# Window attention and two feed-forward layers: the second layer's first product by one level of Strassen's algorithm

## The chip, the core and the metric

The kernel runs on one core of a Trainium2 chip. Its engines have instruction streams of their own and meet at semaphores: TensorE (PE, with its weight loads as PEld) multiplies matrices into PSUM, VectorE (DVE) and ScalarE (ACT) work element by element, GpSimd (POOL) makes constants at the start, and SyncE (SP) issues every DMA transfer. The metric is the device time in microseconds, the median of several runs.

## What is computed

```
q, k, v: (4, 8, 576, 64)     windowed attention, window 64
x = attention output as (2304, 512)
x = relu(x @ w_in1)^2 @ w_out1       w_in1 (512, 2048), w_out1 (2048, 512)
y = elu(x @ w_in2) @ w_out2          w_in2 (512, 2048), w_out2 (2048, 512)
```

q, k and v are 32-bit floats, the four weights 64-bit floats. The output is (2304, 512) in 32-bit floats.

## The kernel before

**Numbers.** Each operand of a large product is split into a high and a low half (`split`, lines 110 to 113: ScalarE writes the high half, VectorE subtracts it for the low one), and each product is three matmuls: high by high, high by low, low by high (`mm3`, lines 289 to 294). Weights come as pairs of 32-bit words. `w_load` (129 to 133) fetches 512 KB for one 128-wide slice, `w_split` (135 to 159) makes a float of it with one ScalarE and four VectorE instructions of 512 columns and splits it. The raw words and the split weight take turns in one buffer, so a load waits for the last matmul that used that buffer.

**Tiles and loops.** The tokens go in five blocks of 512, 256, 512, 512 and 512, numbered 0 to 4. d_ff is cut into 16 slices j. `m_h` (296 to 325) multiplies a block by one slice of w_in into one of two PSUM banks (`ph`), applies the activation (relu squared in layer one; in layer two min on VectorE, exp on ScalarE, max on VectorE) and splits the result into `gs`. `m_out` (327 to 358) adds the slice's part of the second product to four PSUM accumulators (o0 to o3), two slices behind `m_h` (LA = 2). Layer one writes its output to DRAM (`x2d`, through `ev` tiles), layer two reads it back (`x_load`, `x_split`). In layer two the accumulators hold 128 tokens by 512 outputs each, so that block 1, which comes last there (ORDER2), uses two of them.

**Attention** of block t + 1 is done during block t of layer one, a head pair at a time: `u_S` (208 to 245) makes scores, masks, exp and scaling, `u_V` (247 to 269) transposes, multiplies by v and splits into `xs`. The loop spreads it: scores at every third slice, v two slices later. Its loads are issued one head pair ahead.

**Weights by due time.** All weights of layer one are decoded during attention and block 0, those of layer two during block 4 and the first block of layer two; `due` (393 to 397) says how many by when, and `load_w` issues the loads two per slice:

```
    def due(i):

        if i < NJ:
            return min(2 * (LA + 2) + 2 * i, 2 * NJ)
        return 2 * NJ + max(0, (20 * (i - LAST)) // 16)
```

**Order.** The code gives instructions in program order; a scheduler with a timeline of its own then sets the order on each engine, subject to the buffers of each tag (pb 4, pt and ev together 3, y 3, gs 3).

## Time and profile before

| | us |
|---|---|
| median of 3 runs | 891.06 (888.93 to 892.03) |
| profiled run | 890.37 |
| its span, first to last instruction | 888.6 |
| TensorE busy | 870.0 |
| VectorE busy | 503.6 |
| ScalarE busy | 373.8 |
| mean granted TensorE clock | 0.998 of full |

The profiled run has 1.8 us outside its span. The page gives busy times and cuts the span into 40 slices of 22 us; the views by stretch give the same for any interval, with the clock that TensorE was granted. A matmul's own duration includes the way through the array: matmuls overlap, so their cost in a row is read from the starts of groups in the timeline, not from their mean duration.

### The profile page before, as it was taken

To read this page: it belongs to the slowest core of one execution; us is meant where nothing else is said; L and a number is where in the kernel's file an instruction comes from. 1 tells how busy PE (TensorE), PEld (TensorE's weight loads), DVE (VectorE), ACT (ScalarE), POOL (GpSimd) and SP (SyncE) were. 2 spreads that over 40 slices of the span, in tenths; PEclk is the share of its full clock that TensorE was granted. 3 is DMA by queue.
4 is the path that set the end of the run, shared out by engine and by line. 5 is a ranking of instruction groups with operands and counts; after the bars stand their busy time and mean duration, and the time that the engine had idled before them with its cause. 6 is when DMAs were issued, how large, how long until landed. Compare 5 with 4: busy or idle time off the path is not lost.

```text
span 888.6 us, 12491 instructions
## 1 busy us (share of the span) xinstructions
PE 870.0 (98%) x4752; PEld 732.2 (82%) x4752; DVE 503.6 (57%) x1269; ACT 373.8 (42%) x848; POOL 6.9 (1%) x27
## 2 busy tenths in 40 slices
PE   6799999999999999999999999999999999999998
PEld 5488889998888888888888888888888888888897
DVE  6999994435444344444999994543354334433343
ACT  6777765434334243433566542322232223222232
POOL 3000000000000000000000000000000000000000
PEclk9999999999999999999999999999999999999999
DMA  9991212221112111015666400110001000100000
GB/s 267 379 365 38 76 49 78 70 73 50 50 50 56 65 50 49 25 54 185 197 200 195 142 0 1 48 48 1 0 24 48 1 0 1 48 1 0 33 16 24
DMA packets 43835, 67.91 MB, mean 76 GB/s; under 512 B 21504, under 2 KB 24064, under 8 KB 43776
## 3 DMA queue, kind: packets, MB, share of 16 engines
q1 hardware_dynamic: 43776, 67.12, 23.4%
q8 instruction: 37, 0.61, 0.3%
q14 instruction: 22, 0.18, 0.1%
HBM read 57.67 MB, written 9.44 MB: 76 GB/s over the span
## 4 chain that ended last, share of the span: by engine, by line
PE 96%; DVE 3%; DMA 0%; issue 0%; SPq 0%
PE ph L292 44%; PE o L292 44%; PE pa L218 3%; PE pa L264 2%; PE pa L256 1%; DVE pb L242 1%; PE po L218 1%; DVE pb L226 1%; DVE y L154 0%; DVE y L151 0%; DMA kr<-in_k_dram 0%; DVE w L113 0%; DVE xs L113 0%; DVE y L144 0%; DVE y L147 0%
## 5 line engine op out<-in xcount | busy, mean ns | idle before, releaser
L292 PE MATMUL ph<-xs,w 128*128 128x512 f32 (+1 forms) x1920 | 434.0, 371 | 3.7 <-ACT xs L112 2.1
L292 PEld LDWEIGHTS ph<-xs,w 128*128 128x128 f32 x1920 | 336.8, 189 | 66.3 <-ACT xs L112 2.4
L292 PE MATMUL o<-gs,w 128*128 128x512 f32 (+1 forms) x960 | 215.3, 371 | 0.0
L292 PE MATMUL o<-w,gs 128*128 128x512 f32 x864 | 209.6, 389 | 0.0
L292 PEld LDWEIGHTS o<-gs,w 128*128 128x128 f32 x960 | 166.9, 188 | 29.0
L292 PEld LDWEIGHTS o<-w,gs 128*128 128x128 f32 x864 | 161.1, 188 | 32.7
L113 DVE TENSOR_TENSOR gs<-g,gs 128x512 fp32r<-128x512 f32 (+1 forms) x160 | 101.9, 637 | 73.0 <-ACT gs L112 72.8
L112 ACT ACTIVATE gs<-g 128x512 fp32r<-128x512 f32 (+1 forms) x160 | 93.8, 588 | 85.7 <-DVE g L321 55.7
L320 ACT ACTIVATE g<-g 128x512 f32<-128x512 f32 (+1 forms) x80 | 47.1, 589 | 192.5 <-DVE g L317 192.5
L317 DVE TENSOR_SCALAR g<-ph 128x512 f32<-128x512 f32 (+1 forms) x80 | 51.0, 638 | 100.5 <-PE ph L292 100.3
L311 ACT ACTIVATE g<-ph 128x512 f32<-128x512 f32 (+1 forms) x80 | 44.1, 554 | 96.5 <-PE ph L292 95.8
L315 DVE TENSOR_TENSOR g<-g 128x512 f32<-128x512 f32 (+1 forms) x64 | 39.9, 624 | 69.3 <-ACT g L311 69.2
L321 DVE SCALAR_TENSOR_TENSOR g<-g,ph 128x512 f32<-128x512 f32 (+1 forms) x80 | 50.7, 634 | 46.3 <-ACT g L320 46.3
L231 ACT ACTIVATE pb<-pb,nm 128x128 f32<-128x128 f32 x144 | 55.9, 390 | 23.3 <-DVE nm L226 23.2
L143 ACT ACTIVATE y<-wraw 128x512 f32<-128x512 f32 x64 | 42.6, 672 | 25.8 <-DVE w L113 18.5
L112 ACT ACTIVATE w<-y 128x512 fp32r<-128x512 f32 x64 | 39.9, 628 | 17.4 <-DVE y L154 17.3
L113 DVE TENSOR_TENSOR w<-y,w 128x512 fp32r<-128x512 f32 x64 | 43.8, 686 | 0.2 <-ACT w L112 0.2
L151 DVE SCALAR_TENSOR_TENSOR y<-wraw,y 128x512 uint32<-128x512 uint32 x64 | 43.6, 687 | 0.1
L154 DVE SCALAR_TENSOR_TENSOR y<-wraw,y 128x512 uint32<-128x512 uint32 x64 | 43.4, 686 | 0.1
L113 DVE TENSOR_TENSOR xs<-pa,xs 128x512 fp32r<-128x512 f32 (+1 forms) x20 | 12.7, 636 | 42.9 <-ACT xs L112 42.8
L242 DVE TENSOR_SCALAR pb<-pb,rc 128x128 f32<-128x128 f32 x144 | 31.6, 282 | 0.7
L218 PEld LDWEIGHTS pa<-kr,qd 128*128 128x128 f32 x224 | 28.6, 191 | 1.8
(36 smaller groups left out, 368.8 us busy)
## 6 DMA issues: line engine op xcount, KB each, us to landing
wraw<-in_moe_w_in_dram SPq DMA_DIRECT2D x32, 512.0 KB, 5.0
wraw<-in_moe_w_out_dram SPq DMA_DIRECT2D x32, 512.0 KB, 5.3
vr<-in_v_dram SPq DMA_DIRECT2D x16, 512.0 KB, 4.1
out_dram<-ev SPq DMA_DIRECT2D x18, 256.0 KB, 2.1
qd<-in_q_dram SPq DMA_DIRECT2D x32, 128.0 KB, 3.3
x2d<-ev SPq DMA_DIRECT2D x16, 256.0 KB, 2.5
xr<-x2d SPq DMA_DIRECT2D x8, 512.0 KB, 3.5
kr<-in_k_dram SPq DMA_DIRECT2D x12, 288.0 KB, 3.4
```

Source lines behind the costliest of these rows:

```text
L112: nc.scalar.activation(out=hi, in_=x, func=AF.Copy)
L113: eng.tensor_tensor(out=lo, in0=x, in1=hi.bitcast(F32), op=ALU.subtract)
L143: nc.scalar.activation(out=yf, in_=upper.bitcast(F32), func=AF.Abs)
L151: nc.vector.scalar_tensor_tensor(out=y, in0=upper, scalar=0xC0000000, in1=y, op0=ALU.bitwise_and, op1=ALU.bitwise_or)
L154: nc.vector.scalar_tensor_tensor(out=y, in0=lower, scalar=29, in1=y, op0=ALU.logical_shift_right, op1=ALU.bitwise_or)
L218: nc.tensor.matmul(out=ps[:, i * P:(i + 1) * P], lhsT=qr[:, b0 + i].rearrange("p a x -> p (a x)"), rhs=kr[:, o:o + P], start=True, stop=True,)
L231: nc.scalar.activation(out=pb[:, c], in_=pb[:, c], func=AF.Exp, bias=nm[:, b:b + 1], scale=-1.0, accum_out=sm[:, b:b + 1],)
L292: nc.tensor.matmul(out=ps, lhsT=a[x], rhs=b[y], start=(first and i == 0), stop=(last and i == 2))
L311: nc.scalar.activation(out=g[:, :n], in_=ps[:, :n], func=AF.Relu)
L317: nc.vector.tensor_scalar(out=g[:, :n], in0=ps[:, :n], scalar1=0.0, scalar2=None, op0=ALU.min)
L320: nc.scalar.activation(out=g[:, :n], in_=g[:, :n], func=AF.Exp)
L321: nc.vector.scalar_tensor_tensor(out=g[:, :n], in0=g[:, :n], scalar=-1.0, in1=ps[:, :n], op0=ALU.add, op1=ALU.max)
```

## The change

The first product of layer two is computed with the Winograd form of Strassen's algorithm, one level. The tokens of layer two now go in three stripes s of 768, each of two halves of 384 (HALF). d_model is halved too, and a pair i of slices (2i, 2i + 1) makes the two halves of the third dimension. For each of 3 x 8 pairs, seven products of (256 x 128) by (256 x 384) take the place of eight. A product is two chunks of 128 by three matmuls of 384 columns: 24 x 42 = 1008 matmuls of 384 columns, where there were 768 of 512 and 192 of 256. The second product has as many columns as before, all in matmuls of 512.

- **Weight side.** `w_sums(r)` makes the seven left operands of a pair: it decodes two w_in slices, makes four sums of 256 columns, splits seven operands and writes them to DRAM (`wop`), 1.83 MB a pair. It is called eight times in layer one, every six slices from block 1 on; the raw slices and the operands share two "stage" buffers of 512 KB. `wo_load` brings a pair's operands back for each stripe, in the buffers of the attention's `xs`.
- **Token side.** `x_sums` and `x_op` make the seven right operands of a stripe in the buffers of layer one's w_in; for stripe 0 in block 4, for a later one in the last pair of the stripe before.
- **The pair.** Seven products go through two PSUM banks. ScalarE copies the first and the third result, VectorE adds the others up with u2 and u3, which use the "y" buffers of the decode. Four results (384 tokens by 128) go through the activation. The 36 output matmuls of a pair stand between the products of the next one; six accumulators are used (o0 to o3 and the two attention banks). The outputs of layer one's last two slices stand between the products of pair (0, 0).
- **Buffers.** pb 4 to 3, pt with ev 3 to 2, y 3 to 2. The decode of w_out of layer two is due one slice of weights per j in block 4, and the last ones in pair (0, 0).

```diff
-ORDER2 = [0, 2, 3, 4, 1]
+HALF = 384
...
-        y = sc.tile([P, KD * P], U32, tag="y", name="y", bufs=3)
+        y = sc.tile([P, KD * P], U32, tag="y", name="y", bufs=2)
...
+    def w_sums(i):
...
+        add, sub = ALU.add, ALU.subtract
+        H = KD * P // 2
+        y0, y1 = w_float(1, 2 * i, 0), w_float(1, 2 * i + 1, 0)
+        a11, a12, a21, a22 = y0[:, :H], y0[:, H:], y1[:, :H], y1[:, H:]
...
+        nc.vector.tensor_tensor(out=s1, in0=a21, in1=a22, op=add)
+        nc.vector.tensor_tensor(out=s2, in0=s1, in1=a11, op=sub)
+        nc.vector.tensor_tensor(out=a21, in0=a11, in1=a21, op=sub)
+        nc.vector.tensor_tensor(out=s4, in0=a12, in1=s2, op=sub)
+        for k, xs_ in enumerate(((a11, s2), (a12, a21), (s1, a22), (s4,))):
+            n = len(xs_)
+            w = wts.tile([P, 2, 2, 2, P], F32R, tag="stage", name="wo", bufs=2)
...
+            nc.sync.dma_start(out=wop[i][k][:, :n], in_=w[:, :n].bitcast(F32))
...
+    def wo_load(s, i):
...
+            w = xp.tile([P, 2, 2, 2, P], F32R, tag=f"xs{k}", name="wo")
+            nc.sync.dma_start(out=w[:, :n].bitcast(F32), in_=wop[i][k][:, :n])
...
-            pb = at.tile([P, 4 * P], F32, tag="pb", name="pb", bufs=4)
+            pb = at.tile([P, 4 * P], F32, tag="pb", name="pb", bufs=3)
...
-            pt = at.tile([P, 512], F32, tag="pt", name="pt", bufs=3)
+            pt = at.tile([P, 512], F32, tag="pt", name="pt", bufs=2)
...
+    def x_op(s, k):
...
+            src = (b11, t2[c], b21, b12, t1[:, c, :], b21, b22)[k]
+            o = wts.tile([P, 2, HALF], F32R, tag=f"w{2 * k + c}0", name="xo")
+            split(o[:, 0, :], o[:, 1, :], src, nc.vector)
...
+                e = at.tile([P, 512], F32, tag="pt", name="ev", bufs=2)
...
+        a = bank()
+        product(a, 0, A11, True, True)
+        m1 = keep("pb", 3)
+        copy(m1, a[:, :HALF], nc.scalar)
+        after(0)
+        b = bank()
+        product(b, 1, S2, True, True)
+        u2 = plus(keep("y", 2, sc), b, m1)
+        after(1)
+        product(a, 2, A12, False, True)
+        c = keep("pb", 3)
+        copy(c, a[:, :HALF], nc.scalar)
+        out[0, 0] = elu(c)
+        after(2)
+        b = bank()
+        product(b, 3, S3, True, True)
+        u3 = plus(keep("y", 2, sc), b, u2)
+        after(3)
+        a = bank()
+        product(a, 4, S1, True, True)
+        out[1, 1] = elu(plus(keep("pb", 3), a, u3))
+        after(4)
+        product(b, 5, A22, False, True)
+        out[1, 0] = elu(plus(keep("pb", 3), b, u2))
+        after(5)
+        product(a, 6, S4, False, True)
+        out[0, 1] = elu(plus(keep("pb", 3), a, u2))
+        after(6)
...
-    wseq = [(L, j, i) for L in range(2) for j in range(NJ) for i in range(2)]
+    wseq = [(0, j, i) for j in range(NJ) for i in range(2)] + [(1, j, 1) for j in range(NJ)]
...
-        return 2 * NJ + max(0, (20 * (i - LAST)) // 16)
+        return 2 * NJ + max(0, i - LAST)
...
+        if i < len(its) - 2:
+            for f in outs:
+                f()
+        else:
+            left += outs
+        if t == NB - 1:
+            load_w(2 * NJ + j)
+            if j == 0:
+                x_load(0)
+                wo_load(0, 0)
+            elif j == 1:
+                x_sums(0)
+            if j >= 2:
+                x_op(0, (j - 2) // 2) if j % 2 == 0 else None
...
+        r, m = divmod(i - NJ, 6)
+        if r in range(NI):
+            if m == 0:
+                w_load(1, 2 * r, 0)
+            elif m == 2:
+                w_load(1, 2 * r + 1, 0)
+            elif m == 5:
+                w_sums(r)
...
+    for s in range(NS):
+        for i in range(NI):
+            if (s, i) != (NS - 1, NI - 1):
+                wo_load(*divmod(s * NI + i + 1, NI))
+            if s + 1 < NS and i == 3:
+                x_load(s + 1)
+            if s + 1 < NS and i == NI - 1:
+                x_sums(s + 1)
...
+            def after(k, s=s, i=i, fs=left):
+                for f in spread(fs, k):
+                    f()
+                if s == 0 and i == 0:
+                    decode(wd[0] + 1)
+                if s + 1 < NS and i == NI - 1:
+                    x_op(s + 1, k)
...
+            left = pair_out(s, i, pair(s, i, after))
```

Three places show what the scheduler makes of it. In the rows, a name's number tells buffers apart; "x3" stands for three such instructions; what a row waits for is in brackets.

TensorE at the start of layer two, before. ph_4908 is the slice's first product, o0 to o3 the accumulators of the first block, gs_4762 the activation of slice 0:

```order
L292 MATMUL o0_4874<-w_4222,gs_4762 128x512 [waits DVE_49]
L292 MATMUL o2_4876<-w_4222,gs_4762 128x512
L292 MATMUL o1_4875<-w_4222,gs_4762 128x512 [waits DVE_49]
L292 MATMUL o1_4875<-w_4222,gs_4762 128x512 x2
L292 MATMUL ph_4908<-xs_4244,w_4413 128x512 [waits DVE_49]
L292 MATMUL ph_4908<-xs_4244,w_4413 128x512 x2
L292 MATMUL ph_4908<-xs_4388,w_4413 128x512 x3
L292 MATMUL ph_4908<-xs_4532,w_4413 128x512 x3
```

TensorE there after; the last outputs of layer one's slices are past. ph_5221 and ph_5209 are the two banks, and their rows the fifth, sixth and seventh product of pair (0, 0); xo are the token operands, wo the weight operands, gs_5203 the pair's first activation:

```order
L377 MATMUL o0_5291<-w_4573,gs_5203 128x512 [waits DVE_49]
L377 MATMUL o1_5292<-w_4573,gs_5203 128x512
L377 MATMUL o2_5293<-w_4573,gs_5203 128x512
L377 MATMUL ph_5221<-xo_4971,wo_4523 128x384 [waits DMAHW2_49,DVE_49]
L377 MATMUL ph_5221<-xo_4971,wo_4523 128x384 x2
L377 MATMUL ph_5221<-xo_4974,wo_4523 128x384 x3
L377 MATMUL ph_5209<-xo_5062,wo_4523 128x384 [waits DVE_49]
L377 MATMUL ph_5209<-xo_5062,wo_4523 128x384 x2
L377 MATMUL ph_5209<-xo_5066,wo_4523 128x384 x3
L377 MATMUL ph_5221<-xo_5122,wo_4525 128x384 [waits DMAHW3_49,DVE_49]
```

The outputs of the first activation still come first, but no output stands between the products that follow: three come in a row, each behind a wait for VectorE.

VectorE at the start of layer two, before. y is the float of a weight in the making, g the activation:

```order
L151 SCALAR_TENSOR_TENSOR y_5066<-wraw_4637,y_5066 128x512 [waits DVE_49]
L113 TENSOR_TENSOR w_5031<-y_5025,w_5031 128x512 [waits Activation_49]
L317 TENSOR_SCALAR g_4863<-ph_4850 128x512 [waits PE_49]
L144 TENSOR_SCALAR y_5075<-y_5075 128x512 [waits Activation_49]
L113 TENSOR_TENSOR gs_4807<-g_4806,gs_4807 128x512 [waits Activation_49]
L154 SCALAR_TENSOR_TENSOR y_5066<-wraw_4637,y_5066 128x512 [waits DVE_49]
L144 TENSOR_SCALAR y_5116<-y_5116 128x512 [waits Activation_49]
L147 TENSOR_SCALAR y_5075<-y_5075 128x512 [waits DVE_49]
L321 SCALAR_TENSOR_TENSOR g_4863<-g_4863,ph_4850 128x512 [waits Activation_49]
```

VectorE there after. y_5170 is the last w_out slice in the making, y_5186 is u2 and y_5216 is u3:

```order
L163 SCALAR_TENSOR_TENSOR y_5139<-wraw_5137,y_5139 128x512 [waits DVE_49]
L153 TENSOR_SCALAR y_5170<-y_5170 128x512 [waits Activation_49]
L156 TENSOR_SCALAR y_5170<-y_5170 128x512 [waits DVE_49]
L119 TENSOR_TENSOR w_5145<-y_5139,w_5145 128x512 [waits Activation_49]
L160 SCALAR_TENSOR_TENSOR y_5170<-wraw_5148,y_5170 128x512 [waits DMAHW2_49,DVE_49]
L465 TENSOR_TENSOR y_5186<-ph_5179,pb_5165 128x384 [waits DVE_49]
L163 SCALAR_TENSOR_TENSOR y_5170<-wraw_5148,y_5170 128x512 [waits DVE_49]
L119 TENSOR_TENSOR w_5176<-y_5170,w_5176 128x512 [waits Activation_49]
L465 TENSOR_TENSOR y_5216<-ph_5209,y_5186 128x384 [waits DVE_49,PE_49]
```

Before, the activation's steps and those of the decode alternate. After, u2 stands behind three steps of the decode of wraw_5148, u3 behind two more.

TensorE at the end of block 1, before, from just behind the last head pair's products with v. xs_2261 is that pair's result, ph_2338 and ph_2369 the first products of block 2, o0_1636 to o3_1639 the outputs of block 1:

```order
L292 MATMUL ph_2338<-xs_1909,w_395 128x512
L292 MATMUL ph_2338<-xs_2085,w_395 128x512 x3
L292 MATMUL o0_1636<-gs_2290,w_1411 128x256
L292 MATMUL o0_1636<-gs_2290,w_1411 128x256 [waits DVE_49]
L292 MATMUL o0_1636<-gs_2290,w_1411 128x256
L292 MATMUL o1_1637<-gs_2290,w_1411 128x256 x3
L292 MATMUL o2_1638<-gs_2290,w_1411 128x256 x3
L292 MATMUL o3_1639<-gs_2290,w_1411 128x256 x3
L292 MATMUL ph_2369<-xs_1733,w_568 128x512 [waits Activation_49]
L292 MATMUL ph_2369<-xs_1733,w_568 128x512 x2
L292 MATMUL ph_2369<-xs_1909,w_568 128x512 x3
L292 MATMUL ph_2338<-xs_2261,w_395 128x512 [waits Activation_49]
```

TensorE there after. xs_2340 is the last head pair's result, pa the attention's banks, ph_2458 the first product of block 2:

```order
L377 MATMUL o2_1670<-gs_2441,w_1492 128x256
L377 MATMUL o3_1671<-gs_2441,w_1492 128x256 x3
L304 MATMUL pa_2309<-ident_81,pb_2212 128x128 [waits DVE_49] x4
L304 MATMUL pa_2316<-ident_81,pb_2232 128x128 [waits DVE_49]
L312 MATMUL pa_2323<-pt_2314,vr_2022 64x64 [waits DMAHW0_49,Activation_49]
L312 MATMUL pa_2323<-pt_2314,vr_2022 64x64 x7
L304 MATMUL pa_2316<-ident_81,pb_2232 128x128 [waits DVE_49] x3
L312 MATMUL pa_2323<-pt_2321,vr_2022 64x64 [waits Activation_49]
L312 MATMUL pa_2323<-pt_2321,vr_2022 64x64 x7
L266 MATMUL pa_2562<-kr_2200,qd0_84 128x128 [waits DMAHW3_49,DMAHW4_49,DMAHW2_49,PE_49]
L266 MATMUL pa_2562<-kr_2200,qd0_84 128x128 x3
L377 MATMUL ph_2458<-xs_2340,w_427 128x512 [waits Activation_49]
```

Before, twelve matmuls of outputs and ten of products stood between the last head pair's v products and the first use of its result. After, only the next scores (pa_2562) do, and the outputs of block 1 stand ahead of the head pair's transposes.

## Rows read from the trace of the kernel before

**Rows 1.** The page: busy time of the engines, then 40 slices of the span: tenths of VectorE busy, and GB/s moved by DMA.
```profile
PE 870.0 (98%) x4752; PEld 732.2 (82%) x4752; DVE 503.6 (57%) x1269; ACT 373.8 (42%) x848; POOL 6.9 (1%) x27
...
DVE  6999994435444344444999994543354334433343
...
GB/s 267 379 365 38 76 49 78 70 73 50 50 50 56 65 50 49 25 54 185 197 200 195 142 0 1 48 48 1 0 24 48 1 0 1 48 1 0 33 16 24
```

**Rows 2.** Busy time by stretch: from and to, length, busy us (and instructions) of PE, PEld, DVE, ACT and POOL, granted clock of TensorE, share of the DMA engines, GB/s.
```profile
10.00:20.00 10.00, 7.19 (x75) 6.18 (x75) 9.63 (x67) 9.27 (x40) 0.00 (x0) 1.00 1.11 309
...
30.00:40.00 10.00, 8.02 (x82) 5.30 (x78) 10.00 (x27) 5.67 (x11) 0.00 (x0) 1.00 1.04 385
...
50.00:60.00 10.00, 10.00 (x46) 8.29 (x45) 10.00 (x25) 5.98 (x14) 0.00 (x0) 1.00 1.03 414
...
90.00:100.00 10.00, 10.00 (x47) 8.28 (x47) 9.96 (x25) 6.56 (x13) 0.00 (x0) 1.00 0.11 34
...
200.00:300.00 100.00, 100.00 (x602) 83.91 (x601) 42.28 (x151) 39.08 (x112) 0.00 (x0) 1.00 0.18 50
...
430.00:500.00 70.00, 70.00 (x310) 57.99 (x309) 69.54 (x134) 43.04 (x73) 0.00 (x0) 1.00 0.63 198
```

**Rows 3.** Waits of TensorE over the whole span: what waited, for what, us in total, times, longest.
```profile
PE po L218 <- DMA kr<-in_k_dram: 7.2, 3, 5.8
PE ph L292 <- ACT xs L112: 2.1, 2, 1.4
```

**Rows 4.** Timeline of TensorE in layer two, 499 to 510 us: start, length from the first start to the last end, and the group.
```profile
501.40 2.88 PE L292 MATMUL ph<-xs,w 128*128 128x512 f32 x12
504.12 3.56 PE L292 MATMUL o<-w,gs 128*128 128x512 f32 x15
```

**Rows 5.** The same view in layer two's last block, of 256 tokens.
```profile
862.02 1.60 PE L292 MATMUL ph<-xs,w 128*128 128x256 f32 x12
863.45 1.55 PE L292 MATMUL o<-w,gs 128*128 128x512 f32 x6
864.84 1.60 PE L292 MATMUL ph<-xs,w 128*128 128x256 f32 x12
```

**Rows 6.** TensorE's groups by form, both layers: busy us, mean ns of one, idle before.
```profile
L292 PE MATMUL ph<-xs,w 128*128 128x512 f32 x1536 | 380.8, 393 | 3.7 <-ACT xs L112 2.1 <-DVE xs L113 1.1 <-DVE w L113 0.5
L292 PE MATMUL o<-w,gs 128*128 128x512 f32 x864 | 209.6, 389 | 0.0
...
L292 PE MATMUL ph<-xs,w 128*128 128x256 f32 x384 | 53.3, 285 | 0.0
```

**Rows 7.** Groups by form of VectorE, then of ScalarE, same columns.
```profile
L113 DVE TENSOR_TENSOR gs<-g,gs 128x512 fp32r<-128x512 f32 x128 | 88.4, 691 | 58.5 <-ACT gs L112 58.2
...
L144 DVE TENSOR_SCALAR y<-y 128x512 f32<-128x512 f32 x64 | 26.8, 423 | 5.0 <-ACT y L143 4.8
...
L226 DVE CUSTOM_DVE_ANT_0 pb<-pa,mask 128x128 f32<-128x128 f32 x112 | 25.8, 286 | 4.2 <-PE pa L218 4.1
L113 DVE TENSOR_TENSOR gs<-g,gs 128x256 fp32r<-128x256 f32 x32 | 13.6, 425 | 14.6 <-ACT gs L112 14.6
```
```profile
L112 ACT ACTIVATE gs<-g 128x512 fp32r<-128x512 f32 x128 | 80.6, 631 | 73.3 <-DVE g L321 47.5 <-DVE g L315 25.3
...
L143 ACT ACTIVATE y<-wraw 128x512 f32<-128x512 f32 x64 | 42.6, 672 | 25.8 <-DVE w L113 18.5 <-DMA wraw<-in_moe_w_out_dram 5.9 <-DMA wraw<-in_moe_w_in_dram 1.3
...
L117 ACT ACTIVATE pt<-pa 128x512 f32<-128x512 f32 x36 | 20.6, 596 | 5.0 <-PE pa L256 3.8 <-DMA x2d<-ev 1.0
L112 ACT ACTIVATE gs<-g 128x256 fp32r<-128x256 f32 x32 | 13.3, 415 | 12.4 <-DVE g L321 8.2 <-DVE g L315 3.3 <-PE o L292 0.9
```

**Rows 8.** DMA issues between 415 and 500 us: count, KB each, median us from issue to landing.
```profile
wraw<-in_moe_w_out_dram SPq DMA_DIRECT2D x16, 512.0 KB, 4.3
...
xr<-x2d SPq DMA_DIRECT2D x2, 512.0 KB, 7.5
```

**Rows 9.** The same over the whole span.
```profile
out_dram<-ev SPq DMA_DIRECT2D x18, 256.0 KB, 2.1
```

**Rows 10.** TensorE by the microsecond, 40 to 45 us: length, busy us (matmuls), granted clock, share of the DMA engines, GB/s.
```profile
40.00:41.00 1.00, 0.15 (x1) 1.00 1.18 294
41.00:42.00 1.00, 1.00 (x3) 0.58 0.97 221
42.00:43.00 1.00, 1.00 (x3) 0.50 0.95 315
43.00:44.00 1.00, 1.00 (x4) 0.50 1.06 401
44.00:45.00 1.00, 1.00 (x5) 0.71 0.88 329
```

**Rows 11.** Timeline of the tail, all engines.
```profile
880.37 4.27 PE L292 MATMUL o<-w,gs 128*128 128x512 f32 x18
...
884.68 0.69 DVE L119 COPY ev<-o 128x512 f32<-128x512 f32 x1 [1.74 <-PE o L292]
885.07 0.81 SPq L358 DMA_DIRECT2D out_dram<-ev  x2
```

**Rows 12.** Timeline of VectorE in block 0, in a head pair's scores.
```profile
131.28 0.17 DVE L236 TENSOR_SCALAR rc<-sm 128x4 f32<-128x4 f32 x1 [0.48 <-ACT pb L231]
...
131.70 0.87 DVE L242 TENSOR_SCALAR pb<-pb,rc 128x128 f32<-128x128 f32 x4
```

**Rows 13.** The page, costliest groups: weight loads of the first products.
```profile
L292 PEld LDWEIGHTS ph<-xs,w 128*128 128x128 f32 x1920 | 336.8, 189 | 66.3 <-ACT xs L112 2.4
```

More of the change, by code (lines that the diff above doesn't have):

```diff
@@ L289, in mm3, with x_load @@
-    def mm3(ps, a, b, first, last):
+    def x_load(s):
+        b0, b1, tl = 2 * HALF * s, 2 * HALF * (s + 1), []
+        for c in range(KD):
+            if c % 2:
+                x = qd[c // 2].rearrange("p b a x -> p (b a x)").rearrange("p (h n) -> p h n", h=2)
+            else:
+                x = at.tile([P, 2, NMAX], F32, tag="vr", name="xr", bufs=2)
+            for h in range(2):
+                lo, hi = b0 + h * HALF, b0 + (h + 1) * HALF
+                for t, n in enumerate(BLOCKS):
+                    u, v_ = max(lo, T0[t]), min(hi, T0[t] + n)
+                    if u < v_:
+                        nc.sync.dma_start(
+                            out=x[:, h, u - lo:v_ - lo], in_=x2d[t][:, c, u - T0[t]:v_ - T0[t]]
+                        )
+            tl.append(x)
+        xr[s] = tl
@@ new lines, in m_h, with m_out, one @@
+        nc.scalar.activation(out=g[:, :n], in_=ps[:, :n], func=AF.Relu)
+        if t == 0:
+            nc.scalar.activation(out=g[:, :n], in_=g[:, :n], func=AF.Square)
+        else:
+            nc.vector.tensor_tensor(out=g[:, :n], in0=g[:, :n], in1=g[:, :n], op=ALU.mult)
+        split(s[:, 0, :n], s[:, 1, :n], g[:, :n], nc.vector)
+        gs[0, t, j] = s
+    def m_out(t, j):
+        n = BLOCKS[t]
+        w = wt[0, j, 1]
+        g = gs.pop((0, t, j))
+        if j == 0:
+            acc[0] = [ps_o.tile([P, 512], F32, tag=f"o{m}", name=f"o{m}") for m in range(KD)]
+        def one(m, ps):
+            mm3(
+                ps[:, :n],
+                [w[:, r, m * P:(m + 1) * P] for r in range(2)],
+                [g[:, r, :n] for r in range(2)],
+                j == 0, j == NJ - 1,
+            )
+            if j == NJ - 1:
+                e = at.tile([P, 512], F32, tag="pt", name="ev", bufs=2)
+                copy(e[:, :n], ps[:, :n], nc.vector if m % 2 else nc.scalar)
+                nc.sync.dma_start(out=x2d[t][:, m, :], in_=e[:, :n])
+        return [lambda m=m, ps=ps: one(m, ps) for m, ps in enumerate(acc[0])]
@@ new lines, in pair, with product, bank, keep @@
+    def pair(s, i, after):
+        add = ALU.add
+        def product(ps, k, op, first, last):
+            w, x = wo[s, i][op[0]], xo[s, k]
+            for c in range(2):
+                mm3(
+                    ps[:, :HALF], [w[:, op[1], c, r, :] for r in range(2)],
+                    [x[c][:, r, :] for r in range(2)], first and c == 0, last and c == 1,
+                    skip_group_check=True,
+                )
+        def bank():
+            return ps_h.tile([P, 512], F32, tag="h", name="ph")
+        def keep(tag, bufs, pool=at):
+            return pool.tile([P, HALF], F32, tag=tag, name=tag, bufs=bufs)
+        def plus(out, ps, x):
+            nc.vector.tensor_tensor(out=out, in0=ps[:, :HALF], in1=x, op=add)
+            return out
+        out = {}
+        a = bank()
[26 more added lines that the diff above has]
+        after(6)
+        return out
@@ new lines, in window_attention_then_two_mlps, with pair_out, one @@
+    MT = HALF // P
+    def pair_out(s, i, g4):
+        if i == 0:
+            acc[1] = [ps_o.tile([P, 512], F32, tag=f"o{m}", name=f"o{m}") for m in range(KD)]
+            acc[1] += [ps_a.tile([P, 512], F32, tag="a", name="oa") for _ in range(2 * MT - KD)]
+            seen.clear()
+        def one(jj, h, m, g):
+            ps, n = acc[1][h * MT + m], h * MT + m
+            w = wt[1, 2 * i + jj, 1]
+            seen[n] = seen.get(n, 0) + 1
+            mm3(
+                ps, [g[:, r, m * P:(m + 1) * P] for r in range(2)], [w[:, r, :] for r in range(2)],
+                seen[n] == 1, seen[n] == NJ,
+            )
+            if seen[n] == NJ:
+                e = at.tile([P, 512], F32, tag="pt", name="ev", bufs=2)
+                copy(e, ps, nc.vector if n % 2 else nc.scalar)
+                r0 = s * 2 * HALF + n * P
+                nc.sync.dma_start(out=out[r0:r0 + P, :], in_=e)
+        return [lambda jj=jj, h=h, m=m, g=g: one(jj, h, m, g)
+                for (jj, h), g in g4.items() for m in range(MT)]
@@ L361, in window_attention_then_two_mlps @@
+    seen = {}
     order = [(t, p) for t in range(NB) for p in range(HP)]
@@ L387, in o_alloc @@
         return ps_o.tile([P, 512], F32, tag=f"o{rot[0] % KD}", name="po")
-    its = [(0, t, j) for t in range(NB) for j in range(NJ)]
-    its += [(1, t, j) for t in ORDER2 for j in range(NJ)]
+    its = [(t, j) for t in range(NB) for j in range(NJ)]
     LAST = NJ * (NB - 1)
+    NS = NT // (2 * HALF)
+    NI = NJ // 2
     def due(i):
@@ L418, in window_attention_then_two_mlps @@
         m_h(*its[i])
-    for i, (L, t, j) in enumerate(its):
+    left = []
+    for i, (t, j) in enumerate(its):
         if i + LA < len(its):
             m_h(*its[i + LA])
-        if L == 0 and t + 1 < NB:
+        if t + 1 < NB:
             p, r = divmod(j, 3)
```

142 lines of the change are left out of this document (71 added, 71 removed).

## The prediction

> **What bounds the kernel now.** I read the busy table of the page first. TensorE is busy 870.0 of 888.6 us, VectorE 57%, and the slices show VectorE full in two places only: in the first ninth of the span and around 430 to 500 us [rows 1]. The table by stretch says what that means: at 10 to 40 us TensorE waits (7.19 and 8.02 busy of 10), from 50 us it is full (10.00 of 10), at 430 to 500 us too, where VectorE is busy 69.54 of 70 [rows 2]. The waits that end last for TensorE are loads and attention at the start, 7.2 and 2.1 us being the largest [rows 3]. So from 50 us to the tail every TensorE microsecond removed is a microsecond gained, as long as nothing makes TensorE wait. That condition is the whole question here.
>
> **The matmuls.** Twelve products of 512 columns start 2.72 us before the next group, 0.2267 us each [rows 4]. Twelve of 256 columns take 1.43 us, 0.119 each, and the six of 512 behind them 1.39 us, 0.03 more than 6 x 0.2267 = 1.36 [rows 5]. The trace has no 384 columns; halfway between is 0.173, an estimate. Layer two before: 64 slices of 512 tokens x 24 x 0.2267 = 348.2, and 16 of 256 tokens x (1.43 + 1.39) = 45.1, together 393.3 us (the counts of forms agree [rows 6]). After: 24 pairs x (42 x 0.173 + 36 x 0.2267) = 24 x 15.43 = 370.3. A pair goes from narrow to wide about 7 times; at half of the 0.03 that is 2.5 us in 24 pairs, between 0 and 5. **Gain 20.5 us, 18 to 23.** All of it is on the path.
>
> The Trainium skill ("TensorE: Matmul & The Clock Gate", section "Back-to-back issue gap") gives a gap of N / 2.4 ns plus 2.5: 215.8 ns at 512 columns and 109.2 at 256. This trace has some 11 and 10 ns more at both. By the page 384 columns would be 162.5 ns and the sum 1008 x 10.5 ns = 10.6 us lower; the measurement decides.
>
> **A steady pair** costs nothing more. VectorE has 17 operations of 384 columns; between 0.691 (512) and 0.425 (256) lies 0.56, so 9.5 us at most, ScalarE 10 x 0.52 = 5.2 [rows 7], against 15.4 us of TensorE. The longest chain (copy, min, exp, max, two splits: 3.2 us and five hand-overs) has two to three products and their outputs as cover. Without that cover each 0.3 us exposed would be 7 us in 24 pairs.
>
> **Weight operands.** A w_sums call is two decodes of 2 x 0.42 + 2 x 0.69 = 2.2, four sums and seven splits of 256 columns, 11 x 0.42: 9.1 us of VectorE, 73 us in 8 calls. Before, sixteen decodes and splits of the same weights stood in the last block. In blocks 1 to 3 VectorE is busy less than half of the time (42.28 of 100 at 200 to 300 us [rows 2]), so most of it is free. The reads, 1.83 MB in 15.4 us, are 119 GB/s, and 195 to 200 GB/s stand in the page without a wait [rows 1]; nothing for them.
>
> **Start of layer two: 8.0 us lost.** Call T the end of layer one's last matmul. In the new order VectorE's u2 of pair (0,0) (the first L465) stands behind three operations of the last w_out decode, since both use the "y" buffers, and TensorE's fifth product (ph_5221) needs the bank that u2 reads. That decode's load waits for the matmul at T, and stands in SP's queue behind two evictions of layer one's output: issued about T + 1.3 (two copies of 0.6 to 0.69). It lands 4.3 us later, the median of such loads in this stretch [rows 8]. Then abs 0.67, two of 0.42, one split and one of 0.69, u2 0.56, hand-overs 0.3 [rows 7]: u2 ends at T + 9.3. TensorE has for this time one product (1.04) and nine outputs (2.04): it stands from T + 3.1, **6.2 us**. u3 stands behind two more operations (0.69 + 0.69 + 0.56), so the sixth product waits another 1.1, and the first gs chain 0.4: 7.7, taken as 8.0. If the load lands in 2.1, as an output does [rows 9], it is 6; if it takes the 7.5 of the x2d reload in this stretch [rows 8], 11.
>
> **Clock.** After an idle 0.85 us at 40 to 41 the granted clock went to 0.58, 0.50, 0.50, 0.71 of full [rows 10]: the lower level, 1.2 GHz, for some three microseconds, 1.7 us lost. The many waits before 40 us cost no clock. So a 6 us wait costs 0 to 1.7; I take **0.9**. The Trainium skill (same page, "The HAM clock gate") has an idle array fall to the lower level as a rule; by it the term would be 1.7 at the start of layer two and 1.7 at the change of block below, and the sum 2.5 higher.
>
> **Tail: 3.5 us lost.** Before, two accumulators are left at the end: the matmuls end at 884.64, the copy runs from 884.68 for 0.69, the span ends at 888.6 [rows 11], 3.96 after the last matmul. Copy plus landing (2.1 [rows 9]) is 2.8, so 1.1 goes to the issue and the end. Now there are six accumulators and two "ev" buffers: three rounds of 2.8. The first can begin 9 x 0.2267 = 2.04 before the last matmul: 8.4 + 1.1 - 2.04 = 7.5 after it. Bounds 2.5 and 4.5, from the 0.81 of a double issue either way.
>
> **Block 0: 2.5 us lost.** pb goes from 4 to 3 buffers, pt and y from 3 to 2. VectorE's order changes: ahead of the gs of slice 13 there are now 8 more mask steps, 8 more scalings, four small ones and an xs split, and two decode steps less. Scalings come four in 0.87 [rows 12]; masks alike: 2 x 1.7 + 0.7 + 0.69 - 1.4 = 3.4 us more. VectorE is full here (9.96 of 10 at 90 to 100 us [rows 2]), so it can't be made up, but part of it is margin of gs. 0 to 7, since fewer buffers can couple the engines further.
>
> **End of block 1: 3.5 us lost.** The last head pair of block 2 now stands at the very end of block 1, behind w_sums(0) and (1). From its last scores: four masks 0.95, exp 0.6, rc 0.35, four scalings 0.87, transposes 0.4, pt 0.6, V 0.4, two splits 1.3, hand-overs 0.4: 5.9 us [rows 7, 12]. TensorE has 1.4 us of matmuls and 1.2 of attention for it; then its next row wants xs_2340. 3.3, taken as 3.5. Where the order before had the same step, twelve matmuls of outputs and ten of products stood in between. 1 (ScalarE ahead) to 7 (k and v late).
>
> **Two changes of stripe: 2.5 us lost.** In the last pair of a stripe VectorE has some 18 more operations, 35 x 0.56 = 19.6 us at most against 15.4, and ScalarE's splits of the new x stand before the exp that the next output needs. I follow VectorE's order there and get 1.3 us for each. 0 to 5.
>
> **The sum** against the profiled run: 890.4 - 20.5 + 8.0 + 0.9 + 3.5 + 2.5 + 3.5 + 2.5 = **890.8 us**. The profiled run lies 0.7 under the median of three (891.06), less than the runs scatter. So the matmuls saved are given back at the edges of the stages. The bounds of the terms, combined loosely, give 883 to 898 for this case.
>
> **Rivals.** (1) The cover holds: only the matmuls and the tail count, 890.4 - 20.5 + 3.5 = 873.4. For it: TensorE had no gap at 430 to 500 us beside a VectorE that was full [rows 2]. Against it: the waits above follow from the order on each engine, and at T a load stands between. 0.18.
> (2) Slower: the SP queue in layer one. The four writes of each w_sums, and the loads of w_in that wait for one of two "stage" buffers, stand ahead of the loads of the next attention. If a k or v load is issued later than its head pair's turn, the last head pair comes late at all three changes of block behind block 1, not at one: 3 x 4.5 instead of 3.5 gives 900.8. It decides when a write holds the queue for longer than the one head pair that is loaded ahead. For it: 14.7 MB of writes that were not there. Against: the DMA engines are busy 0.18 at 200 to 300 us [rows 2]. 0.15.
> (3) A 384-column matmul goes at the pace of its weight load, 0.189 [rows 13]: 1008 x 0.016 = 16 us, 907. Against: 256 columns run at 0.119 with loads of the same length. 0.05.
>
> **Chances.** The forecast has 0.62. A measurement of this kernel tells 0.3% from no change: under 888.4 is faster, over 893.7 slower. Of the forecast's 0.62, 0.23 lie below, 0.20 within, 0.19 above. With rival 1 faster is 0.41, with 2 and 3 slower is 0.39, same 0.20. Its own range is 883 to 898; 8 in 10 reaches from 873 (half of rival 1) to 901 (half of rival 2).
>
> **What would show it.** Spacing of 384 columns near 0.173 and a steady pair of 15.5 us: the gain. One gap of 6 us in TensorE before the fifth product of layer two, ended by VectorE's L465, with the last w_out load in front of it. Six evictions in three rounds, 7.5 us behind the last matmul. A gap of 3 to 4 us at the end of block 1, ended by an xs split. If layer two takes 372 us with only the tail gap, rival 1 is right; gaps at each change of block with loads as releaser are rival 2. Gaps inside steady pairs would make the forecast wrong in a way that I priced at nothing.

## The result, and the profile after

The changed kernel takes 901.9 us (median of 4, 900.67 to 902.58), the kernel before 891.27 in the same session: a ratio of 1.0122 (1.0105 to 1.014). It is slower by 1.2%, and lies 3.9 us above the forecast's own range of 883 to 898 and 0.9 above the wide one of 873 to 901. The profiled run has a span of 900.7 us, 12.1 more than before. Three executions further down, one each of the kernel before, b_pb and a_noload, took 1423 to 3574 us, and the medians leave them out.

The page of the changed kernel, the same three lines as in [rows 1]:

```profile
PE 866.0 (96%) x4800; PEld 747.7 (83%) x4800; DVE 589.4 (65%) x1555; ACT 414.7 (46%) x990; POOL 6.9 (1%) x27
...
DVE  6999997777577764444788764556845458554554
...
GB/s 276 368 390 72 72 26 147 164 161 179 173 163 178 170 154 49 42 45 140 100 120 133 265 106 117 106 121 124 242 117 133 114 108 134 161 137 107 114 27 71
```

TensorE is busy 4 us less, not 20, and has 34.7 us of idle time where it had 18.6. The busy time by stretch, columns as in [rows 2], shows where:

```profile
80.00:100.00 20.00, 18.17 (x114) 14.47 (x113) 17.87 (x52) 14.54 (x37) 0.00 (x0) 1.00 0.31 82
100.00:120.00 20.00, 19.39 (x111) 15.86 (x109) 19.00 (x61) 15.39 (x40) 0.00 (x0) 1.00 0.24 70
120.00:140.00 20.00, 18.64 (x86) 14.65 (x87) 18.53 (x38) 11.29 (x20) 0.00 (x0) 1.00 0.00 1
...
200.00:300.00 100.00, 98.06 (x583) 81.47 (x582) 71.67 (x251) 54.41 (x160) 0.00 (x0) 0.97 0.50 165
300.00:400.00 100.00, 100.00 (x596) 83.56 (x595) 52.50 (x176) 43.25 (x122) 0.00 (x0) 1.00 0.30 97
...
500.00:520.00 20.00, 13.87 (x61) 11.30 (x60) 15.04 (x29) 7.38 (x13) 0.00 (x0) 0.93 0.66 218
520.00:540.00 20.00, 20.00 (x94) 18.39 (x93) 11.33 (x24) 6.95 (x14) 0.00 (x0) 0.90 0.36 119
```

Block 0 (80 to 140 us) loses 3.8 us of idle time that was not there before. Around 200 us TensorE waits, and its clock falls. At 500 to 540 us 6.1 us are idle and the clock costs 20 x 0.07 + 20 x 0.10 = 3.4. The rest of layer two is full up to the tail, but for one wait at the first change of stripe:

```profile
636.19 0.73 PE L377 MATMUL o<-w,gs 128*128 128x512 f32 x2 [1.42 <-ACT gs L118]
```

The timeline of the start of layer two:

```profile
508.68 0.38 SPq L142 DMA_DIRECT2D wraw<-in_moe_w_out_dram  x1
...
509.92 2.31 PE L377 MATMUL o<-w,gs 128*128 128x512 f32 x9 [0.88 <-ACT gs L118]
...
513.27 0.66 ACT L152 ACTIVATE y<-wraw 128x512 f32<-128x512 f32 x1 [2.92 <-DMA wraw<-in_moe_w_out_dram]
...
513.97 0.43 DVE L153 TENSOR_SCALAR y<-y 128x512 f32<-128x512 f32 x1 [1.45 <-ACT y L152]
514.43 0.43 DVE L156 TENSOR_SCALAR y<-y 128x512 uint32<-128x512 uint32 x1
514.77 0.69 DVE L119 TENSOR_TENSOR w<-y,w 128x512 fp32r<-128x512 f32 x1
515.37 0.69 DVE L160 SCALAR_TENSOR_TENSOR y<-wraw,y 128x512 uint32<-128x512 uint32 x1
515.97 0.55 DVE L465 TENSOR_TENSOR y<-ph,pb 128x384 f32<-128x384 f32 x1
...
516.58 1.84 PE L377 MATMUL ph<-xo,wo 128*128 128x384 f32 x6 [4.35 <-DVE y L465]
...
518.70 0.56 DVE L465 TENSOR_TENSOR y<-ph,y 128x384 f32<-128x384 f32 x1
...
519.31 1.01 PE L377 MATMUL ph<-xo,wo 128*128 128x384 f32 x2 [0.90 <-DVE y L465]
```

Here the forecast can be read line by line: the last w_out load is issued at 508.68, ScalarE waits until 513.27 for it, u2 (the first L465) stands behind three steps of that decode and a split of the weight before it, and the fifth product waits 4.35 us for it, the sixth 0.90 for u3. The first outputs wait 0.88 us for their activation. Products in a row, and then a steady pair (809.66 to 825.38), in the same kernel:

```profile
565.45 2.26 PE L377 MATMUL ph<-xo,wo 128*128 128x384 f32 x12
567.54 1.55 PE L377 MATMUL o<-w,gs 128*128 128x512 f32 x6
...
809.66 1.21 PE L377 MATMUL ph<-xo,wo 128*128 128x384 f32 x6
810.71 0.39 PE L377 MATMUL o<-w,gs 128*128 128x512 f32 x1
810.94 0.63 PE L377 MATMUL oa<-w,gs 128*128 128x512 f32 x2
811.41 1.22 PE L377 MATMUL ph<-xo,wo 128*128 128x384 f32 x6
812.47 2.24 PE L377 MATMUL o<-w,gs 128*128 128x512 f32 x9
814.55 1.23 PE L377 MATMUL ph<-xo,wo 128*128 128x384 f32 x6
...
819.80 1.55 PE L377 MATMUL o<-w,gs 128*128 128x512 f32 x6
821.18 1.21 PE L377 MATMUL ph<-xo,wo 128*128 128x384 f32 x6
...
825.38 1.21 PE L377 MATMUL ph<-xo,wo 128*128 128x384 f32 x6
```

Twelve products in a row take 2.09 us (0.174 each), six between outputs 1.05. From the first product of a pair to that of the next it is 15.71 us in the last six pairs; 24 of them are 377.0 us, against 393.3 before. The tail:

```profile
891.33 6.73 SPq L520 DMA_DIRECT2D out_dram<-ev  x6
...
892.55 0.61 PE L377 MATMUL oa<-w,gs 128*128 128x512 f32 x2
893.48 0.60 ACT L123 ACTIVATE ev<-o 128x512 f32<-128x512 f32 x1 [2.17 <-DMA out_dram<-ev]
...
897.01 0.69 DVE L125 COPY ev<-oa 128x512 f32<-128x512 f32 x1 [2.17 <-DMA out_dram<-ev]
```

The matmuls end at 893.16, the span 7.5 us later; before it was 3.96 [rows 11]. Each later round waits for a transfer.

Between the stages it helps to follow one matmul: the start, in each profiled run, of the matmul that begins the n-th twelve of the layer-one products (12 x 4 twelves further is four slices), in us from the start of the span.

```
                    before  change  b_buf  a_stage  a_hold  a_fix  a_best
block 1, slice 4     143.0   148.7  152.3   152.7   148.4   142.7  143.7
block 2, slice 4     216.1   226.3  226.0   230.6   222.1   219.1  217.3
block 3, slice 4     319.2   332.5  329.1   336.8   331.1   328.0  322.8
block 4, slice 0     398.7   412.1  408.7   416.9   411.6   407.5  402.9
```

The change is 5.6 us behind at block 1, 10.2 at block 2 and 13.3 at block 4. But the mark of block 2 does not stand behind the same work everywhere: in the change, a_stage and a_fix (in a_half and a_noload too) eight output matmuls of 512 columns (8 x 0.2267 = 1.8 us) that stood ahead of it before stand behind it; in b_buf, a_hold and a_best they do not. With the same work counted, the change loses 6.4 us between the marks of block 1 and block 2, and 1.3 from there to block 4. The 6.4 us are seen at the end of block 1:

```profile
207.69 0.33 PE L304 MATMUL pa<-ident,pb 128*128 128x128 f32 x1 [0.98 <-DVE pb L290]
...
209.79 1.02 PE L312 MATMUL pa<-pt,vr 128*64 128x64 f32 x16 [0.69 <-ACT pt L123]
...
213.10 1.22 PE L377 MATMUL ph<-xs,w 128*128 128x512 f32 x2 [0.27 <-ACT xs L118]
```

These waits are 1.9 us, all in the chain of the last head pair; the clock behind them costs 3.4 (last section); 1.0 shows as neither. No wait and no fall of the clock stands between the mark of block 2 and block 4.

The account of the span: matmuls -16.3, up to block 1 +5.6, end of block 1 +6.4, blocks 2 and 3 +1.3, start of layer two +9.5, changes of stripe +1.9 (from the second pair's start to the last one's it is 347.5 us, where 22 steady pairs are 345.6), tail +3.5: 11.9 of the 12.1 us.

### The profile page after: what moved, and what is told of

The parts are those of the page before. It is cut to its first block, busy times and chain, and to the rows that moved or that the text cites. A ratio compares the mean times of both kernels' runs of the same rounds, so it can differ in the third digit from the quotient of the medians.

```text
span 900.7 us, 13414 instructions
## 1 busy us (share of the span) xinstructions
PE 866.0 (96%) x4800; PEld 747.7 (83%) x4800; DVE 589.4 (65%) x1555; ACT 414.7 (46%) x990; POOL 6.9 (1%) x27
## 4 chain that ended last, share of the span: by engine, by line
PE 89%; DVE 5%; DMA 2%; ACT 1%; issue 1%; POOL 0%; SPq 0%; DVEq 0%; POOLq 0%; ACTq 0%
PE ph L377 40%; PE o L377 35%; PE oa L377 7%; PE pa L266 3%; PE pa L312 2%; PE pa L304 1%; DVE y L160 1%; DVE pb L274 1%; DVE pb L290 1%; PE po L266 1%; DMA wraw<-in_moe_w_in_dram 1%; DMA wraw<-in_moe_w_out_dram 1%; DVE w L119 1%; DVE y L163 0%; DMA out_dram<-ev 0%
## 5 line engine op out<-in xcount | busy, mean ns | idle before, releaser
L377 PE MATMUL ph<-xs,w 128*128 128x512 f32 (+1 forms) x960 | 224.9, 377 | 7.4 <-ACT w L118 2.2
L377 PE MATMUL ph<-xo,wo 128*128 128x384 f32 x1008 | 203.6, 340 | 5.3 <-DVE y L465 5.3
L377 PEld LDWEIGHTS ph<-xs,w 128*128 128x128 f32 x960 | 167.4, 190 | 40.8 <-DVE w L119 3.2
L377 PEld LDWEIGHTS ph<-xo,wo 128*128 128x128 f32 x1008 | 182.5, 190 | 19.3 <-DVE y L465 6.2
L118 ACT ACTIVATE gs<-g 128x384 fp32r<-128x384 f32 (+2 forms) x176 | 96.9, 552 | 82.1 <-DVE g L434 51.1
L119 DVE TENSOR_TENSOR gs<-g,gs 128x384 fp32r<-128x384 f32 (+2 forms) x176 | 103.5, 590 | 37.4 <-ACT gs L118 36.6
L377 PEld LDWEIGHTS o<-w,gs 128*128 128x128 f32 x576 | 106.9, 188 | 17.8 <-ACT gs L118 2.9
L377 PE MATMUL oa<-w,gs 128*128 128x512 f32 x288 | 84.4, 393 | 0.0
L434 DVE SCALAR_TENSOR_TENSOR g<-g,pb 128x384 f32<-128x384 f32 x96 | 53.1, 555 | 27.5 <-ACT g L433 27.5
L152 ACT ACTIVATE y<-wraw 128x512 f32<-128x512 f32 x64 | 42.8, 668 | 49.5 <-DMA wraw<-in_moe_w_out_dram 18.6
L377 PEld LDWEIGHTS oa<-w,gs 128*128 128x128 f32 x288 | 53.9, 188 | 10.2
L465 DVE TENSOR_TENSOR pb<-ph,y 128x384 f32<-128x384 f32 x72 | 40.1, 556 | 22.8 <-PE ph L377 22.1
```

The costliest lines, as they stand in the source:

```text
L118: nc.scalar.activation(out=hi, in_=x, func=AF.Copy)
L119: eng.tensor_tensor(out=lo, in0=x, in1=hi.bitcast(F32), op=ALU.subtract)
L152: nc.scalar.activation(out=yf, in_=upper.bitcast(F32), func=AF.Abs)
L377: nc.tensor.matmul(out=ps, lhsT=a[x], rhs=b[y], start=(first and i == 0), stop=(last and i == 2), **kw,)
L434: nc.vector.scalar_tensor_tensor(out=e, in0=e, scalar=-1.0, in1=c, op0=ALU.add, op1=ALU.max)
L465: nc.vector.tensor_tensor(out=out, in0=ps[:, :HALF], in1=x, op=add)
```

## The experiments

**The buffer cuts alone.** The kernel before, with nothing but

```diff
-            pb = at.tile([P, 4 * P], F32, tag="pb", name="pb", bufs=4)
+            pb = at.tile([P, 4 * P], F32, tag="pb", name="pb", bufs=3)
...
-            pt = at.tile([P, 512], F32, tag="pt", name="pt", bufs=3)
+            pt = at.tile([P, 512], F32, tag="pt", name="pt", bufs=2)
...
-        y = sc.tile([P, KD * P], U32, tag="y", name="y", bufs=3)
+        y = sc.tile([P, KD * P], U32, tag="y", name="y", bufs=2)
```

(ev like pt), and then each cut by itself: pb in `b_pb`, y in `b_y`, pt and ev in `b_pt`.

b_buf: 

> The kernel before with the change's buffer cuts alone: pb 4 to 3, pt and ev 3 to 2, y 3 to 2. In the changed kernel the first product of block 1's steady part (its slice 4) starts 5.6 us later than before. Theory A, the cuts cost this: 5 to 6 us more than before, all of it between 80 and 150 us, and nothing behind. Rival B, the first w_sums and the attention behind it cost it: under 1.5 us.

b_pb: 

> The kernel before with pb at 3 buffers instead of 4, nothing else. All cuts together cost 8 us, all of it in block 0 and the attention ahead of it. Theory A, pb is the one that couples scores and v (a head pair holds two pb until its transposes): 5 us or more. Rival B, the decode's y or the evictions' pt is: under 2 us.

b_y: 

> The kernel before with y at 2 buffers instead of 3, nothing else. Theory A, pb is the dear one: under 2 us here. Rival B, the decode, which fills VectorE up to 60 us, needs the third y so that ScalarE's abs and the split of two weights overlap: 4 us or more.

b_pt: 

> The kernel before with pt and ev at 2 buffers instead of 3, nothing else. All cuts together cost 8 us, y alone 4.4, pb alone 2.5 in the medians. If the three add up: 1 us. Rival, pt is in the chain of every head pair (transposes, copy, v), and the three overlap: 3 us or more.

Measured: all three 899.12 against 891.16 (ratio 1.0094, 1.0058 to 1.013), y alone 894.96 against 890.61 (1.0049, 1.0032 to 1.0066), pb alone 892.78 (1.0023, 1.0008 to 1.0038), pt alone 891.46 against 891.63 (1.0002, 0.9992 to 1.0012). The cuts cost 8 us, more than theory A's 5 to 6, all by block 1 (9.3 in the profiled run) and hardly anything behind. TensorE's order up to block 1's slice 4 is that of the change; of the 9.3 us 3.4 are clock that the change did not lose there, and without them it is 5.9 against the change's 5.6. The y of the decode is the dear one, and I had expected pb, whose 2.2 us fit neither theory; the sum of the single cuts, 4.4 + 2.2 - 0.2 = 6.4, is most of the whole. What waits is seen in b_buf's waits of TensorE, and in its timeline:

```profile
PE ph L292 <- ACT w L112: 2.0, 2, 1.2
...
PE ph L292 <- DVE w L113: 1.6, 2, 1.1
...
97.20 0.67 ACT L143 ACTIVATE y<-wraw 128x512 f32<-128x512 f32 x1 [0.91 <-DVE w L113]
...
99.88 0.73 PE L292 MATMUL ph<-xs,w 128*128 128x512 f32 x2 [0.76 <-ACT w L112]
...
101.69 4.14 PE L292 MATMUL ph<-xs,w 128*128 128x512 f32 x10 [1.07 <-DVE w L113]
```

TensorE waits for weights, which it did for 0.5 us before [rows 6]: with two y, ScalarE's abs of a weight waits until VectorE's split of an earlier one is done.

**The last load off the path.** The last two w_out slices are loaded first, into the two stage buffers, which are idle in block 4 (in the whole edit these become two tags of one buffer each, taken in turn):

```diff
+        if L and i and j >= NJ - 2:
+            return dict(tag=f"stage{j % 2}", bufs=1)
...
-    wseq = [(0, j, i) for j in range(NJ) for i in range(2)] + [(1, j, 1) for j in range(NJ)]
+    wseq = [(0, j, i) for j in range(NJ) for i in range(2)] + [(1, j % NJ, 1) for j in range(NJ - 2, 2 * NJ - 2)]
```

a_stage: 

> The changed kernel with the raw words of the last two w_out slices of layer two in the stage buffers, which are free in block 4, and fetched first, so that no load waits for the end of layer one. Theory A, that load is what TensorE waits for at the start of layer two (0.88, 4.35 and 0.90 us idle, and a granted clock of 0.93 and 0.90 for 40 us, worth 3.4): 7 to 9.5 us less, the first pair near 21 us from its first product to the next pair's, not 25.92. Rival B, u2 waits for a y buffer and VectorE's queue in any case: under 3 us less.

894.03 us (ratio to before 1.0041), 7.9 less than the change, as theory A has it; the first pair takes 16.05 us, less than the 21 expected. The idle time at 500 to 540 us falls to 0.73 and the clock stays up; u2 now stands ahead of the last decode:

```profile
500.00:520.00 20.00, 19.27 (x95) 16.80 (x94) 15.55 (x30) 8.55 (x17) 0.00 (x0) 1.00 0.73 258
520.00:540.00 20.00, 20.00 (x101) 18.06 (x100) 11.35 (x24) 7.40 (x15) 0.00 (x0) 1.00 0.36 119
```

**The tail.** Two more tags for the last evictions:

```diff
-                e = at.tile([P, 512], F32, tag="pt", name="ev", bufs=2)
+                tag = ("pt", "pt", "kr", "kr", "vr", "vr")[n] if s == NS - 1 else "pt"
+                e = at.tile([P, 512], F32, tag=tag, name="ev", bufs=2)
```

a_tail: 

> The changed kernel with six buffers for the last stripe's six evictions, two each from three tags, so that no copy waits for a transfer. Theory A, three rounds of copy and transfer make the tail 7.5 us long where it was 4.1: 3 us less, 4.3 to 5 us from the last matmul to the end. Rival B, six transfers of 256 KB share the queue and land late: 1 us less or no change.

899.12 us, 2.8 less; the six issues take 3.48 us where they took 6.73, with no wait for a transfer.

**w_sums later.** `a_late` moves the calls by sixteen slices in the code (`divmod(i - 2 * NJ, 6)`), `a_hold` keeps a_stage, calls every four slices, and ties both stage buffers until block 2's first activation.

a_late: 

> The changed kernel with the eight calls of w_sums one block later (from the first slice of block 2 on, not of block 1). In the changed kernel block 2 comes 7 us further behind, at its first slices, where ScalarE stands at a decode of w_sums that waits for its load. Theory A, the calls in the short block 1 cost these 7 us: 5 to 8 us less than the changed kernel, block 3 starting 5 to 6 us behind the kernel before and not 13.3. Rival B, it is the buffer cuts or the calls as such: block 4 starts as late as in the changed kernel, and the time is within 2 us.

a_hold: 

> The kernel with the last w_out slices in the stage buffers, and the first loads of w_sums tied to the activation of block 2's first slice, so that nothing of w_sums stands in block 1, and a call every four slices. That kernel without the tie starts block 4 some 8 us behind the buffer-cut kernel before (18.2 and 9.9 behind the kernel before). Theory A, ScalarE's decode waiting for its load at the end of block 1, ahead of the last head pair's split, costs 4 to 5 of it, and VectorE's load the rest: block 4 starts 10 to 12 us behind the kernel before, and the time falls by 5 to 8 us. Rival B, the work of w_sums costs the same wherever it stands: block 4 starts within 2 us of 18.

a_late: 923.77 us, a miss of both theories. The timeline shows the first operand split in block 1 all the same, and a wait for VectorE's L465 in the first pair of layer two, with the last calls around it:

```profile
145.03 0.43 DVE L119 TENSOR_TENSOR wo<-y,wo 128x256 fp32r<-128x256 f32 x1
...
542.41 1.01 PE L377 MATMUL ph<-xo,wo 128*128 128x384 f32 x2 [22.57 <-DVE y L465]
```

The first five calls stay where they were: a later place in the code only pushed the last three to the end of layer one and into layer two (their first splits at 457, 500 and 532 us). With a dependence instead (a_hold) the step to block 2 is gone, and with it the fall of the clock:

```profile
200.00:240.00 40.00, 40.00 (x249) 33.93 (x249) 23.85 (x78) 18.72 (x53) 0.84 (x2) 1.00 0.45 152
```

From slice 4 of block 1 to slice 4 of block 2 it loses 0.6 us, a_stage 6.7 with the same work counted. But then 6.9 us are lost in blocks 2 and 3, where the calls are denser (a_stage 1.8), and the time is 892.5, only 1.5 less than a_stage. Theory A had the place right, and not the gain of 5 to 8 us: block 4 starts 12.9 us behind, where it had 10 to 12 and rival B 16 to 20.

**Three remedies together.** a_stage, a_tail, and buffers borrowed for block 0 from tags that w_sums uses only later:

```diff
+        if L == 0 and turns[0] % 3 == 0:
+            y = wts.tile([P, KD * P], U32, tag="stage0", name="y", bufs=1)
...
+            if t < 2 and turns[1] % 4 == 0:
+                pb = wts.tile([P, 4 * P], F32, tag="stage1", name="pb", bufs=1)
...
+            if t < 2 and turns[2] % 3 == 0:
+                pt = sc.tile([P, 512], F32, tag="ss", name="pt", bufs=1)
```

a_fix: 

> The kernel with the last w_out slices in the stage buffers, with six buffers for the last evictions, and with three buffers borrowed for block 0: every third y of layer one in a stage buffer, every fourth pb of the first two blocks in the other, every third pt there in ss. If each loss stands for itself: 901.9 - 7.9 - 2.8 - 8 = 883 us, ahead of the kernel before (891.2). Rival, the borrowed buffers tie the decode to w_sums, or the losses hide behind each other: 889 us or more.

883.93 us, a ratio of 0.9914 (0.9888 to 0.994), where 883 was expected: the three losses stand for themselves, and slice 4 of block 1 begins as early as before (142.7 us, 143.0 before).

**What is left in blocks 1 to 3.** In a_fix two waits of TensorE stand out, both behind ScalarE held by a DMA:

```profile
206.18 0.38 ACT L123 ACTIVATE ev<-o 128x256 f32<-128x256 f32 x1 [2.95 <-DMA x2d<-ev]
...
208.24 2.13 PE L400 MATMUL ph<-xs,w 128*128 128x512 f32 x6 [2.15 <-ACT g L419]
...
313.06 0.66 ACT L167 ACTIVATE y<-wraw 128x512 f32<-128x512 f32 x1 [4.28 <-DMA wraw<-in_moe_w_in_dram]
...
314.56 2.79 PE L400 MATMUL ph<-xs,w 128*128 128x512 f32 x11 [1.19 <-ACT g L419]
```

So I took the transfers away, on top of the three remedies: `a_noload` decodes a constant, `a_nowrite` writes only the first pair's operands.

a_noload: 

> The kernel with the three remedies (last w_out slices in the stage buffers, six buffers for the last evictions, borrowed buffers in block 0), and without the sixteen loads of layer two's w_in: w_sums decodes a constant, all its other work and its writes stay (the operands are not those of the weights). With the loads this kernel loses 9.2 us between slice 4 of block 1 and block 4. Theory A, ScalarE stands at the decode's abs until its load lands, with the next activation behind it: the loss falls to 5 us or less. Rival B, the loss is the work of w_sums on VectorE and ScalarE: it stays at 8 us or more.

a_nowrite: 

> The same three remedies, and without seven of the eight pairs' writes of operands: the operands of all pairs are made, those of the first are written and read for every pair. Theory A, the writes fill the one queue, so that loads and x2d transfers land late and ScalarE waits for them: of the 9.2 us between slice 4 of block 1 and block 4 no more than 5 stay. Rival B, the loads or the work itself: 8 us or more.

884.06 and 887.47 us: neither is faster than a_fix (883.93). From slice 4 of block 1 to block 4 they lose 6.9 and 9.5 us, a_fix 9.2. For the loads that lies between the two theories, for the writes it is rival B. How much of it is scatter a_third shows (below), whose order in layer one is that of a_fix: it loses 6.3 us there. So no gain from taking either away is shown; both together were not taken away, and without them the order differs. Then by number and by place:

a_half: 

> The three remedies, and only the first four of the eight calls of w_sums (the operands of the first four pairs are read for all eight, so the output is not the reference's). Theory A, the loss comes from the calls that stand beside the last head pairs of block 1: about 4 us late at slice 4 of block 2 as with all eight, and little less at block 4: 4 to 6 us. Rival B, each call costs the same: half of 9, and half of it already gone at block 2: under 3 us there.

a_best: 

> The three remedies, with all eight calls from block 2's first activation on, one every four slices. Theory A: block 1 and the first slices of block 2 lose nothing against the kernel before (under 1 us at slice 4 of block 2), and the dense calls lose 3 to 7 us in blocks 2 and 3: 880 to 884 us. Rival B, the calls cost the same wherever they stand: 9 us lost, 884 us or more.

`a_half` (four calls): 882.32 us, 5.9 us lost up to block 4, 4.6 of them by slice 4 of block 2 with the same work counted (its mark there stands 2.8 behind), which is theory A. `a_best`: 882.42 us, 0.6 us lost up to slice 4 of block 2 and 3.5 up to block 4, a ratio to before of 0.9911 (0.9893 to 0.9929), which is theory A at its lower end. So the calls beside block 1's last head pairs are the dear ones. What the later ones cost is open: from slice 4 of block 2 to block 4 it is 1.3 us in the change, 4.0 in a_fix, and with the calls every four slices 2.9 in a_best and 6.9 in a_hold, each with an order of its own. a_best has the lowest median of the versions that compute the output, 8.8 us under the kernel before; its 1.5 us on a_fix lie within the scatter of both.

**Fewer changes of width.** The outputs of a pair given in three groups (`spread`), on top of a_fix.

a_third: 

> The same three remedies, with the 36 output matmuls of a pair in three groups, behind the second, fourth and sixth product, instead of seven. A pair takes 15.71 us steadily, where 42 x 0.173 + 36 x 0.2267 = 15.43. Theory A, each change from 384 to 512 columns costs 0.03 us: four changes fewer, 15.59 a pair and 3 us less in all. Rival B, products in a row wait for VectorE and ScalarE between them, or the scheduler mixes the groups again: no gain or a loss.

884.7 us, and still 15.71 a pair, with the outputs in seven groups as before: rival B's case, so the price of a change of width is not tested and is left to the timeline. There it is not a fixed 0.03. In the steady pair above three outputs take 0.70 us, nine 2.08 and six 1.38, which is 0.02 to 0.04 more than 0.2267 each, and six products 1.05 where 6 x 0.173 is 1.04.

## Why the prediction was wrong

The forecast said 890.8, no change; it was 901.9. Term by term, in the profiled run:

| step | predicted | measured | shown by |
|---|---|---|---|
| matmuls of layer two | -20.5 | -16.3 | timeline: 15.71 a pair |
| start of layer two, wait | +8.0 | +6.1 | a_stage |
| the clock behind it | +0.9 | +3.4 | a_stage |
| tail | +3.5 | +3.5 | a_tail |
| block 0 | +2.5 | +5.6 (8 in b_buf's median) | b_buf, b_y, b_pb |
| end of block 1 | +3.5 | +3.0 | a_hold, a_best |
| the clock behind it | 0 | +3.4 | a_hold, a_best |
| blocks 2 and 3 | 0 | +1.3 | trace only |
| changes of stripe | +2.5 | +1.9 | trace only |

The failed steps are three. **The clock** is the largest. The forecast priced it once, at 0.9 with a bound of 1.7, from one fall in the trace before; behind the waits at the end of block 1 it put nothing. It fell at both places, for 3.4 us each: 6.8 for 0.9, more than half of the 11 us. Where it falls varies from run to run (last section), how much in all hardly: the mean granted clock is 0.988 to 0.989 in the four executions of the change. **The matmul gain** was off by 4.2 (0.175 a pair). The forecast had 0.1 a pair for changes of width; with the widths in turn the products take 0.11 and the outputs 0.17 more than 0.173 and 0.2267 each, which is the timeline's figure and has no experiment behind it. **Block 0** was priced by the operations that move on VectorE, and its cuts taken as a margin that could be used; it is a loss of its own, since the third y is what lets the decode of one weight overlap the split of another. The bound of 7 was about right, the value taken from it was not.

What held: the start of layer two as a chain of load, decode and u2, which a_stage shows, though the wait was 1.9 shorter than forecast; that its sum with the clock comes to 9.5 for 8.9 is luck, two errors that cancel. The tail; the steady pair with no idle time; the stall at the end of block 1 in size. Its cause is the calls of w_sums beside the last head pairs (a_hold and a_best have no such step), but its sign was not as forecast: of the waits only 0.27 us is for an xs split, the others come earlier in the head pair's chain. w_sums as nearly free behind that held too, at 1.3 us.

Rival 1 is refuted by the 6.1 us of waits at the start of layer two. Rival 2 wanted late k and v loads at three changes of block: no load is what TensorE waits for at the end of block 1, and at the two later changes it has no wait at all. Rival 3 is refuted by the spacing of 0.174.

The Trainium skill ("TensorE: Matmul & The Clock Gate", section "Back-to-back issue gap") gives N / 2.4 + 2.5 ns for the isolated gap at the full clock; worked out for 384 columns that is an estimate of 162.5 ns. This trace does not agree: its products in a row stand 174 ns apart.
